# Pooled attention before two feed-forward stages: the tails of v pooled once per batch, and later groups' probabilities turned by one block transpose and a trip through DRAM

## The chip, the cores and the metric

The kernel runs on one core of one Trainium2 chip. The metric is device microseconds of one launch. Three runs of the kernel before took 1480.33, 1483.54 and 1484.5 us; the median is 1483.54 us.

## What is computed

```python
def _attn_ref(q, k, v):                     # 8 batches, 8 heads, 576 rows, 64 columns, float32
    k_p = k.reshape(B, H, Sp, 8, D).mean(axis=3)      # 72 pooled keys
    v_p = v.reshape(B, H, Sp, 8, D).mean(axis=3)
    scores = scale * np.matmul(q, k_p.transpose(0, 1, 3, 2))
    attn = np.exp(scores - scores.max(-1, keepdims=True))
    attn = attn / (attn.sum(-1, keepdims=True) + 1e-09)
    return np.matmul(attn, v_p)
...
    x = attn_out.transpose(0, 2, 1, 3).reshape(4608, 512)
    x = ((x @ w1) * (x @ w2)) @ w3 @ w_out            # 512 -> 1024 -> 512
    h = x @ w_in                                      # 512 -> 2048
    return (h * sigmoid(1.702 * h)) @ w_out2          # 2048 -> 512
```

Inputs q, k, v are float32; the weights arrive as 64-bit floats and are converted on the chip.

## The kernel before, in words

Every product of a feed-forward stage is taken as three matmuls: an operand is split into a rounded part and a remainder, and `mm3` (lines 112 to 116) multiplies high by high, high by low and low by high. `split` (103 to 105) makes the parts: ACT copies the high part, DVE or POOL subtracts it to get the low part.

**Attention** is cut into 32 groups: group n is batch n // 4 and the pair of heads n % 4. A group goes through these steps:
- `g_load`, `v_load`: SP issues four DMAs of k, four of q (lines 229 to 232), one of v (249, 128 of the 144 pooled rows of the two heads) and one of v's tail (250, the last 16 pooled rows, into `vtr`).
- `g0`: DVE turns k and q in 32x32 blocks (255, 256), sums k over its 8 rows (258); ACT puts the sums into the block-diagonal `kbd`.
- `g1`, `g2`: TensorE makes the scores of 576 queries against 2 x 72 keys (278), DVE takes the maximum and subtracts (283, 285), ACT takes exp (294).
- `g3`: DVE sums, inverts, normalises (300 to 303). The result `s_t` has queries on partitions and 160 key columns (144 and padding). It must be turned so that keys are on partitions, in `p0` (128 keys) and `p1` (the other 16, in 32 partitions). For groups 0 to 3 TensorE turns it (in `g4`); for groups 4 to 31 DVE does, with 20 transposes of 32 partitions each (310 to 316), which also carry each 32x32 block to other partitions.
- `g_va`: POOL sums v over its 8 rows in three halvings (324, 325, 327), once for 128 partitions (`va`) and once for the tail (`vat`), then scales (329 with a mask, 332 for the tail). `g_vb`: ACT and POOL split the sums into `vm` and, for the tail, `vt` (two ACT copies, lines 340 and 341, and one subtraction on POOL, 342).
- `g4`: ACT copies the high parts of `p0` and `p1` (368, 370, 371), POOL makes the low parts (369, 372).
- `g6`: TensorE multiplies by v (380 to 383), ACT and DVE write the split result into the slots `x` of the first feed-forward stage (390, 391).

**Around it.** From the start, weights are converted by `Conv`: SP loads a tile (line 151), ACT, DVE and POOL work on it (166, 168, 169, 172). The product of w3 and w_out is formed meanwhile (508 and `mm3`), and the first groups run among these steps. Then comes a loop over nine blocks of 512 rows and eight slices f: per f, 24 matmuls against w1 and w2 (624), the copy and product of the two (638, 641), a split, and 12 matmuls of the next stage, two slices late (`x2_step`). Twice per f, `tick` advances the attention by a quarter of a group, so that a group takes two values of f; block j needs the groups of batch j complete. The last group ends with block 6. Then the pool of the attention is closed and its memory is reused for converting w_in and w_out2, and from line 670 on the second feed-forward stage runs.

The order in which each engine takes its instructions is fixed when the program is built: the framework orders them by a simulated time line (`schedule_with_timeline_sim=True`), starting from the order of the code. So a later group's steps can stand ahead of an earlier group's on one engine, and each engine, SP's DMA queue too, keeps its order when the chip runs.

Single-buffered tiles that matter here: `vr`, `vtr`, `p0`, `p1`, `s_t` (for groups from 4 on), `kT`, `qT`, `ph`, `pt`; the raw k and q share four buffers.

Of the kernel before, what the change touches and what calls it, by code (L numbers as in the profile page):

```python
# [7 lines left out]
F32 = mybir.dt.float32  # L8
F32R = mybir.dt.float32r
# [3 lines left out]
ALU = mybir.AluOpType  # L13
# [4 lines left out]
P = 128  # L18
# [4 lines left out]
def pooled_attention_moe_moe2(  # L23
# [18 lines left out]
    nc = tc.nc  # L42
    B, H, S, D = q.shape
    NT, DM = out.shape
    POOL = 8
    SK = S // POOL
# [3 lines left out]
    HP = H // 2  # L50
# [18 lines left out]
    dr_p = ctx.enter_context(tc.tile_pool(name="dr", bufs=1, space=DRAM))  # L69
# [121 lines left out]
    with pa_ctx:  # L191
        pa = pa_ctx.enter_context(tc.tile_pool(name="pa", bufs=1))
        cv_p[0] = pa


        mask = pa.tile([P, 2, D], F32, name="mask")
        nc.gpsimd.memset(mask, 1.0 / POOL)
        nc.gpsimd.affine_select(
            out=mask[:, 0], in_=mask[:, 0], compare_op=ALU.is_gt, fill=0.0,
            base=SK, pattern=[[0, D]], channel_multiplier=-1)  # L200
        nc.gpsimd.affine_select(
            out=mask[:, 1], in_=mask[:, 1], compare_op=ALU.is_ge, fill=0.0,
            base=-SK, pattern=[[0, D]], channel_multiplier=1)
# [9 lines left out]
        vtr = pa.tile([32, POOL * D], F32, name="vtr")  # L213
# [11 lines left out]
        g_q, g_k, g_v, g_s = {}, {}, {}, {}  # L225
# [17 lines left out]
        def v_load(n):  # L243
            if n >= NG:
                return
            b, hp = divmod(n, HP)
            vr = v[b, 2 * hp:2 * hp + 2].rearrange("h (s u) d -> (h s) (u d)", u=POOL)
            g_v[n] = pa.tile([P, POOL * D], F32, name="vr", tag="vr")
            nc.sync.dma_start(g_v[n], vr[:P])
            nc.sync.dma_start(vtr[:KT], vr[P:])  # L250

        def g0(n):
            kr, qr = g_k.pop(n), g_q.pop(n)
            kT = pa.tile([P, S], F32, name="kT", tag="kT")
            nc.vector.transpose(out=kT, in_=kr.rearrange("p g d -> p (g d)"))
            nc.vector.transpose(out=qT[:, :S], in_=qr.rearrange("p g d -> p (g d)"))
# [39 lines left out]
        def g3(n):  # L296
            r, s_t = g_s.pop(n), s_of(n)
            pv = s_t[:, :, :KW].rearrange("p t (a s) -> p t a s", s=SK)
            rv = r.rearrange("p (t a) -> p t a", a=2)
            nc.vector.tensor_reduce(out=rv, in_=pv, op=ALU.add, axis=AX.X)  # L300
            nc.vector.tensor_scalar_add(r, r, 1e-9)
            nc.vector.reciprocal(out=r, in_=r)
            nc.vector.tensor_tensor(
                out=pv, in0=pv, in1=rv.unsqueeze(3).to_broadcast([P, TT, 2, SK]), op=ALU.mult)
            p0 = pa.tile([P, TT, P], F32, name="p0", tag="p0")
            p1 = pa.tile([32, TT, P], F32, name="p1", tag="p1")
            g_s[n] = (p0, p1)
            if n < NPE:
                return
            for r in range(5):  # L310
                for c in range(4):
                    nt = TT if 32 * (c + 1) <= S - (TT - 1) * P else TT - 1
                    dst = p0[32 * r:32 * r + 32] if r < 4 else p1[:32]
                    nc.vector.transpose(  # L314
                        out=dst[:, :nt, 32 * c:32 * c + 32],
                        in_=s_t[32 * c:32 * c + 32, :nt, 32 * r:32 * r + 32])

        def g_va(n):

            vr, tr = g_v.pop(n), vtr  # L320
            a = pa.tile([P, 4 * D], F32, name="va", tag="va")
            at = pa.tile([32, 4 * D], F32, name="vat", tag="vat")
            for d, s in ((a, vr), (at, tr)):
                nc.gpsimd.tensor_tensor(out=d, in0=s[:, :4 * D], in1=s[:, 4 * D:], op=ALU.add)
                nc.gpsimd.tensor_tensor(
                    out=d[:, :2 * D], in0=d[:, :2 * D], in1=d[:, 2 * D:], op=ALU.add)
                nc.gpsimd.tensor_tensor(out=d[:, :D], in0=d[:, :D], in1=d[:, D:2 * D], op=ALU.add)
            vf = pa.tile([P, 2, D], F32, name="vf", tag="vf")
            nc.gpsimd.tensor_tensor(
                out=vf, in0=a[:, :D].unsqueeze(1).to_broadcast([P, 2, D]), in1=mask, op=ALU.mult)  # L330
            vtf = pa.tile([32, D], F32, name="vtf", tag="vtf")
            nc.gpsimd.tensor_scalar_mul(vtf, at[:, :D], 1.0 / POOL)
            g_v[n] = (vf.rearrange("p a d -> p (a d)"), vtf)
            v_load(n + 1)

        def g_vb(n):
            vf, vtf = g_v.pop(n)
            nc.scalar.copy(vm[:, 0], vf)
            nc.gpsimd.tensor_tensor(out=vm[:, 1], in0=vf, in1=f32(vm[:, 0]), op=ALU.subtract)
            nc.scalar.copy(vt[:32, D:], vtf)  # L340
            nc.scalar.copy(vt[64:96, D:], vtf)
            nc.gpsimd.tensor_tensor(
                out=vt[32:64, D:], in0=vtf, in1=f32(vt[:32, D:]), op=ALU.subtract)

        def g4(n):
            p0, p1 = g_s.pop(n)
            if n < NPE:
                ps, s_t = banks_of(n), s_of(n)
# [4 lines left out]
                w = S - T  # L353
# [12 lines left out]
            s0 = p0.rearrange("p t c -> p (t c)")[:, :S]  # L366
            s1 = p1.rearrange("p t c -> p (t c)")[:, :S]
            nc.scalar.copy(ph[:, 0], s0)
            nc.gpsimd.tensor_tensor(out=ph[:, 1], in0=s0, in1=f32(ph[:, 0]), op=ALU.subtract)
            nc.scalar.copy(pt[:32], s1)  # L370
            nc.scalar.copy(pt[32:64], s1)
            nc.gpsimd.tensor_tensor(out=pt[64:96], in0=s1, in1=f32(pt[:32]), op=ALU.subtract)

        def g6(n):
            b, hp = divmod(n, HP)
# [296 lines left out]
    with tc.tile_pool(name="pb", bufs=1, reuse_waits="tile") as pb, \  # L672
# [196 lines left out]
        x = x_first  # L869
# [259 lines left out]
```

## Time and profile before

| | |
|---|---|
| median of three runs | 1483.54 us |
| profiled execution, its own time | 1480.04 us |
| span of its instructions | 1478.3 us |
| TensorE (PE) busy in the span | 1437.1 us (97%) |
| VectorE (DVE) busy | 991.5 us (67%) |
| ScalarE (ACT) busy | 696.6 us (47%) |
| GpSimd (POOL) busy | 491.9 us (33%) |
| granted TensorE clock, mean | 0.994 |
| attention's last matmul | about 629 us after the start |

A busy matmul time is modelled and pipelined: two matmuls overlap in it. What ends a stage is therefore read from TensorE's idle time, and not from its busy time alone. In a list of instructions the number in square brackets is the idle time of the engine just before, with what ended it. A line such as 105 belongs to a helper that many steps call.

### The profile page before, as it was taken

The page shows a single profiled execution, that of the slowest core. Times are in us where ns is not written, and L with a number is a line of the kernel's source. Part 1 is how long each engine was busy: PE and PEld are TensorE (multiplying, and loading weights), DVE is VectorE, ACT ScalarE, POOL GpSimd, SP SyncE. Part 2 cuts the span into 40 slices and gives each one's busy share as a digit, 9 for nine tenths or more (in the row PEclk, how much of TensorE's full clock was granted, in tenths as well). Part 3 has the DMA queues.
Part 4 walks back from the last instruction along what each step waited for, and adds up shares of the span by engine and source line. Part 5 has one row for each costly group of instructions (what it writes and reads, how often), then busy time and mean ns, then how long its engine had stood idle before and what let it go on. Part 6 is the DMA issues. An engine that isn't in the chain of part 4 may idle for free.

```text
span 1478.3 us, 19409 instructions
## 1 busy us (share of the span) xinstructions
PE 1437.1 (97%) x6536; PEld 1188.0 (80%) x6536; DVE 991.5 (67%) x1728; ACT 696.6 (47%) x1212; POOL 491.9 (33%) x589
## 2 busy tenths in 40 slices
PE   5978999999999999999999999999999999999998
PEld 3766888888888888888888887888788888888886
DVE  7889998878787877645636345783559354954554
ACT  6974444434343434366635334652455244634442
POOL 8787865555555555357743200000000000000000
PEclk9989999999999999999999999999999999999999
DMA  9992333323232321089869978877677766785665
GB/s 275 243 227 41 65 81 61 77 49 77 47 75 48 74 41 37 29 295 337 329 230 391 330 240 306 292 213 225 200 237 223 224 199 216 241 237 179 196 213 141
DMA packets 294434, 267.63 MB, mean 181 GB/s; under 512 B 201664, under 2 KB 226240, under 8 KB 294336
## 3 DMA queue, kind: packets, MB, share of 16 engines
q1 hardware_dynamic: 291648, 265.09, 60.0%
q10 hardware_dynamic: 2688, 1.31, 0.3%
q8 instruction: 52, 0.85, 0.2%
q14 instruction: 46, 0.38, 0.1%
HBM read 209.72 MB, written 56.62 MB: 180 GB/s over the span
## 4 chain that ended last, share of the span: by engine, by line
PE 82%; DVE 7%; DMA 5%; ACT 2%; POOL 2%; issue 1%; SPq 1%; DVEq 0%; ACTq 0%; POOLq 0%
PE bk L709 39%; PE wk L114 8%; PE wk L116 8%; PE wk L115 8%; PE acc L114 4%; PE acc L115 4%; PE acc L116 4%; PE wk L278 2%; DMA wud<-wt 2%; DVE s L105 1%; DVE cv L169 1%; PE bk L114 1%; PE bk L115 1%; PE bk L116 1%; POOL cv L172 1%
## 5 line engine op out<-in xcount | busy, mean ns | idle before, releaser
L709 PE MATMUL bk<-xM,st 128*128 128x512 f32 x1140 | 269.1, 390 | 1.8 <-DMA st<-wind 1.3
L709 PE MATMUL bk<-mv,st 128*128 128x512 f32 x1104 | 258.7, 389 | 0.5 <-DMA st<-wud 0.5
L709 PEld LDWEIGHTS bk<-xM,st 128*128 128x128 f32 x1140 | 213.6, 188 | 48.0 <-issue 1.9
L709 PEld LDWEIGHTS bk<-mv,st 128*128 128x128 f32 x1104 | 207.1, 188 | 44.2 <-ACT mv L104 0.9
L114 PE MATMUL wk<-s,s 128*128 128x512 f32 x576 | 227.3, 396 | 6.1 <-DVE a L641 4.1
L116 PE MATMUL wk<-s,s 128*128 128x512 f32 x576 | 225.2, 391 | 0.9 <-DVE s L105 0.9
L115 PE MATMUL wk<-s,s 128*128 128x512 f32 x576 | 225.3, 392 | 0.1
L314 DVE STREAM_TRANSPOSE p<-s_t 32x160 f32<-32x160 f32 (+1 forms) x560 | 178.3, 318 | 10.5
L115 PE MATMUL acc<-s,s 128*128 128x512 f32 x352 | 141.2, 401 | 1.0 <-POOL s L105 0.8
L116 PE MATMUL acc<-s,s 128*128 128x512 f32 x352 | 140.7, 400 | 1.6 <-DVE s L105 1.6
L114 PE MATMUL acc<-s,s 128*128 128x512 f32 x352 | 134.1, 406 | 8.1 <-DVE s L105 5.4
L114 PEld LDWEIGHTS wk<-s,s 128*128 128x128 f32 x576 | 108.5, 189 | 30.1 <-DVE a L641 5.4
L116 PEld LDWEIGHTS wk<-s,s 128*128 128x128 f32 x576 | 108.5, 188 | 23.8 <-DVE s L105 1.1
L115 PEld LDWEIGHTS wk<-s,s 128*128 128x128 f32 x576 | 108.5, 188 | 22.1 <-DVE s L391 0.5
L105 POOL TENSOR_TENSOR s<-a,s 128x512 fp32r<-128x512 f32 x56 | 73.3, 1309 | 155.2 <-ACT s L104 121.4
L105 DVE TENSOR_TENSOR mv<-g,mv 128x1024 fp32r<-128x1024 f32 x80 | 97.8, 1222 | 32.5 <-ACT mv L104 31.0
L104 ACT CAST mv<-g 128x1024 fp32r<-128x1024 f32 x80 | 84.5, 1056 | 71.3 <-PE bk L709 70.8
L172 POOL TENSOR_TENSOR cv<-cv,s 128x512 int32<-128x512 int32 x72 | 100.8, 1408 | 33.6 <-DVE cv L169 24.2
L114 PEld LDWEIGHTS acc<-s,s 128*128 128x128 f32 x352 | 67.9, 194 | 23.3 <-ACT s L104 4.7
L116 PEld LDWEIGHTS acc<-s,s 128*128 128x128 f32 x352 | 67.9, 193 | 15.8 <-DVE s L105 2.7
L115 PEld LDWEIGHTS acc<-s,s 128*128 128x128 f32 x352 | 68.0, 193 | 14.4 <-POOL s L105 2.0
L638 ACT COPY a<-wk 128x512 f32<-128x512 f32 x72 | 42.1, 585 | 68.3 <-PE wk L116 68.1
(188 smaller groups left out, 2344.6 us busy)
## 6 DMA issues: line engine op xcount, KB each, us to landing
st<-wud SPq DMA_DIRECT2D x92, 512.0 KB, 4.3
st<-wind SPq DMA_DIRECT2D x66, 512.0 KB, 4.6
st<-wind SPq DMA_DIRECT2D x84, 256.0 KB, 3.8
s<-in_moe_w_dram SPq DMA_DIRECT2D x32, 512.0 KB, 6.5
wind<-s SPq DMA_DIRECT2D x32, 512.0 KB, 5.5
s<-in_moe_w_out_dram SPq DMA_DIRECT2D x24, 512.0 KB, 6.9
s<-wud SPq DMA_DIRECT2D x20, 512.0 KB, 4.3
kr<-in_k_dram SPq DMA_DIRECT2D x128, 72.0 KB, 2.5
```

Source lines behind the costliest of these rows:

```text
L104: nc.scalar.copy(dst[:, 0], src)
L105: lo_eng.tensor_tensor(out=dst[:, 1], in0=src, in1=f32(dst[:, 0]), op=ALU.subtract)
L114: nc.tensor.matmul(o, a[:, 0, a_sl], b[:, 0, b_sl], start=first, stop=False)
L115: nc.tensor.matmul(o, a[:, 0, a_sl], b[:, 1, b_sl], start=False, stop=False)
L116: nc.tensor.matmul(o, a[:, 1, a_sl], b[:, 0, b_sl], start=False, stop=last)
L169: nc.vector.tensor_scalar(out=wu, in0=e.bitcast(U32), scalar1=3, scalar2=None, op0=ALU.logical_shift_left)
L172: nc.gpsimd.tensor_tensor(out=w.bitcast(I32), in0=w.bitcast(I32), in1=lo_w.bitcast(I32), op=ALU.add)
L278: nc.tensor.matmul(sc[half][:, i * KW:(i + 1) * KW], qT[:, sl(tt)], mov, start=True, stop=True)
L314: nc.vector.transpose(out=dst[:, :nt, 32 * c:32 * c + 32], in_=s_t[32 * c:32 * c + 32, :nt, 32 * r:32 * r + 32])
L638: nc.scalar.copy(a, pa_)
L709: nc.tensor.matmul(o, w[:, x, m], b[:, y], start=first and n == 0, stop=last and n == 2, skip_group_check=True)
```

## The change

Two edits. First, the tails of v: one tile `vtr` of 128 partitions holds the tails of all four head pairs of a batch, each in its own 32 partitions. It is loaded by four DMAs at the batch's first group, pooled and split there once, and the later groups of the batch take their 32 partitions from it by three ACT copies per group. The sums of v are now made in place in `vr` and `vtr`, without `va` and `vat`; the mask shrinks to one column per head and is broadcast.

Second, from group 8 on (`NPT` = 8) the 20 transposes of 32 partitions are replaced by one transpose of all 128 partitions, which turns each 32x32 block but leaves it in its partitions; four DMAs write the result to DRAM and two read it back into `p0` and `p1` with keys on partitions. To make this work, `turn_q` places q's blocks in another order with two transposes in place of one, so that columns come in halves (`by_half`). In these groups the low parts of the probabilities are made on DVE and not on POOL.

```diff
-            nc.sync.dma_start(vtr[:KT], vr[P:])
+            if hp == 0:
+                for h in range(HP):
+                    nc.sync.dma_start(
+                        vtr[32 * h:32 * h + KT],
+                        v[b, 2 * h + 1, S - KT * POOL:].rearrange("(s u) d -> s (u d)", u=POOL))
+        NPT = 2 * HP
+        PC = TT * 32
+        def turn_q(n, qr):
+            if n < NPT:
+                nc.vector.transpose(out=qT[:, :S], in_=qr.rearrange("p g d -> p (g d)"))
+                return
+            dst = qT.rearrange("p (t h e j) -> p e h t j", h=2, e=2, j=32)
+            src = qr.rearrange("p (h g) d -> p h g d", h=2)
+            for e, g0_, g1_ in ((0, 0, TT), (1, TT, SB // 2)):
+                nc.vector.transpose(out=dst[:, e, :, :g1_ - g0_], in_=src[:, :, g0_:g1_])
...
-            for r in range(5):
-                for c in range(4):
...
+            if n < NPT:
+                for r in range(5):
+                    for c in range(4):
...
+                return
+            turned = pa.tile([P, 5, TT, 32], F32, name="pT", tag="pT")
+            nc.vector.transpose(
+                out=turned.rearrange("p r t j -> p t r j"),
+                in_=s_t.rearrange("p t (r k) -> p t r k", k=32))
+            d = dr_p.tile([5, 32, 4, PC], F32, name="pD", tag="pD", bufs=2)
+            for c in range(4):
+                nc.sync.dma_start(
+                    d[:, :, c].rearrange("r k x -> k r x"),
+                    turned[32 * c:32 * c + 32].rearrange("p r t j -> p r (t j)"))
+            nc.sync.dma_start(
+                p0.rearrange("p t c -> p (t c)"), d[:4].rearrange("r k c x -> (r k) (c x)"))
+            nc.sync.dma_start(
+                p1.rearrange("p t c -> p (t c)"), d[4].rearrange("k c x -> k (c x)"))
...
-            vr, tr = g_v.pop(n), vtr
-            a = pa.tile([P, 4 * D], F32, name="va", tag="va")
-            at = pa.tile([32, 4 * D], F32, name="vat", tag="vat")
-            for d, s in ((a, vr), (at, tr)):
...
+            vr, first = g_v.pop(n), n % HP == 0
+            for d in (vr, vtr) if first else (vr,):
+                for w in (4 * D, 2 * D, D):
+                    nc.gpsimd.tensor_tensor(
+                        out=d[:, :w], in0=d[:, :w], in1=d[:, w:2 * w], op=ALU.add)
             vf = pa.tile([P, 2, D], F32, name="vf", tag="vf")
...
+            if first:
+                vtf = vtr[:, D:2 * D]
+                nc.gpsimd.tensor_scalar_mul(vtf, vtr[:, :D], 1.0 / POOL)
+                vtq[0] = pa.tile([P, 2, D], F32R, name="vtq", tag="vtq")
+                split(vtq[0], vtf, nc.gpsimd)
...
-            nc.scalar.copy(vt[:32, D:], vtf)
-            nc.scalar.copy(vt[64:96, D:], vtf)
-            nc.gpsimd.tensor_tensor(
-                out=vt[32:64, D:], in0=vtf, in1=f32(vt[:32, D:]), op=ALU.subtract)
+            for i, half in enumerate((0, 1, 0)):
+                nc.scalar.copy(vt[32 * i:32 * i + 32, D:], f32(tail[:, half]))
...
+            late = n >= NPT
+            lo = nc.vector if late else nc.gpsimd
...
+            lo.tensor_tensor(out=by_half(ph[:, 1]), in0=s0, in1=by_half(f32(ph[:, 0])), op=ALU.subtract)
...
+            lo.tensor_tensor(
+                out=by_half(pt[64:96]), in0=s1, in1=by_half(f32(pt[:32])), op=ALU.subtract)
```

## Rows read from the trace of the kernel before

**Rows 1.** Busy time by stage: stretch, its length, each engine's, granted clock, DMA.
```profile
0.00:212.00 212.00, 180.86 (x840) 144.25 (x841) 184.82 (x340) 135.16 (x284) 165.28 (x202) 0.96 0.68 160
212.00:610.00 398.00, 398.00 (x1921) 336.69 (x1920) 320.75 (x786) 157.86 (x352) 209.00 (x297) 1.00 0.26 56
610.00:1478.00 868.00, 858.27 (x3779) 707.09 (x3777) 485.97 (x604) 403.59 (x576) 117.64 (x91) 1.00 0.75 244
```

**Rows 2.** What PE waited for in 0 to 212 us: total, times, longest.
```profile
PE wk L508 <- POOL cv L172: 10.6, 2, 9.2
PE acc L114 <- DVE s L105: 5.4, 3, 2.9
PE wk L114 <- DVE a L641: 4.1, 2, 2.2
```

**Rows 3.** PE in order of time around 81 us: start, duration, idle before.
```profile
81.08 0.61 PE L114 MATMUL acc<-s,s 128*128 128x512 f32 x1 [2.90 <-DVE s L105]
81.49 0.63 PE L115 MATMUL acc<-s,s 128*128 128x512 f32 x1
81.92 0.63 PE L116 MATMUL acc<-s,s 128*128 128x512 f32 x1
```

**Rows 4.** The chain that ended last, the score matmuls of two successive groups.
```profile
399.25 1.23 PE wk L278 x10
417.93 1.23 PE wk L278 x10
```

**Rows 5.** DVE's groups of instructions, 250 to 600 us: busy us, mean ns, idle.
```profile
L314 DVE STREAM_TRANSPOSE p<-s_t 32x160 f32<-32x160 f32 (+1 forms) x378 | 120.4, 319 | 7.5
L255 DVE STREAM_TRANSPOSE kT<-kr 128x576 f32<-128x576 f32 x17 | 13.0, 765 | 0.0
L301 DVE TENSOR_SCALAR nm<-nm 128x10 f32<-128x10 f32 x19 | 3.3, 174 | 0.7
```

**Rows 6.** POOL's groups of instructions, 0 to 212 us.
```profile
L372 POOL TENSOR_TENSOR pt<-p,pt 32x576 fp32r<-32x576 f32 x9 | 13.5, 1504 | 0.9 <-POOL ph L369 0.3
L324 POOL TENSOR_TENSOR vat<-vtr 32x256 f32<-32x256 f32 x11 | 8.4, 764 | 0.2 <-DMA vtr<-in_v_dram 0.2
L325 POOL TENSOR_TENSOR vat<-vat 32x128 f32<-32x128 f32 x11 | 5.3, 484 | 0.0
L332 POOL TENSOR_SCALAR vtf<-vat 32x64 f32<-32x64 f32 x11 | 5.1, 460 | 0.0
L342 POOL TENSOR_TENSOR vt<-vtf,vt 32x64 fp32r<-32x64 f32 x10 | 5.0, 503 | 0.8
L327 POOL TENSOR_TENSOR vat<-vat 32x64 f32<-32x64 f32 x11 | 4.1, 375 | 0.0
```

**Rows 7.** DVE's group of line 301 in 0 to 212 us.
```profile
L301 DVE TENSOR_SCALAR nm<-nm 128x10 f32<-128x10 f32 x10 | 7.6, 764 | 0.2
```

**Rows 8.** One late group in order of time: normalising, last low part, product with v.
```profile
406.68 0.90 DVE L303 TENSOR_TENSOR s_t<-s_t,nm 128x720 f32<-128x720 f32 x1
...
416.53 1.42 POOL L372 TENSOR_TENSOR pt<-p,pt 32x576 fp32r<-32x576 f32 x1
...
425.16 0.29 PE L380 MATMUL wk<-ph,vm 128*128 128x288 f32 x1
```

**Rows 9.** ACT's copies of line 340 in 250 to 600 us.
```profile
L340 ACT CAST vt<-vtf 32x64 fp32r<-32x64 f32 x19 | 4.6, 241 | 0.0
```

**Rows 10.** Four DMA issues of one group's k on SP's queue: start, duration.
```profile
401.70 1.93 SPq L229 DMA_DIRECT2D kr<-in_k_dram  x4
```

**Rows 11.** Landing of the 256 KB stores of tile x2o to DRAM.
```profile
DMA to landing us min/median/max: 2.2/2.6/5.8
```

**Rows 12.** DMA issues of v: count, size, median us to landing.
```profile
vr<-in_v_dram SPq DMA_DIRECT2D x32, 256.0 KB, 2.8
```

**Rows 13.** SP's load of group 5's v, and POOL's last read of group 4's.
```profile
109.24 0.81 SPq L249 DMA_DIRECT2D vr<-in_v_dram  x1
...
114.76 0.45 POOL L329 TENSOR_TENSOR vf<-va,mask 128x128 f32<-128x128 f32 x1
```

More of the change, by code (lines that the diff above doesn't have):

```diff
@@ L193, in pooled_attention_moe_moe2 @@
         cv_p[0] = pa
-        mask = pa.tile([P, 2, D], F32, name="mask")
+        mask = pa.tile([P, 2], F32, name="mask")
         nc.gpsimd.memset(mask, 1.0 / POOL)
         nc.gpsimd.affine_select(
-            out=mask[:, 0], in_=mask[:, 0], compare_op=ALU.is_gt, fill=0.0,
-            base=SK, pattern=[[0, D]], channel_multiplier=-1)
+            out=mask[:, 0:1], in_=mask[:, 0:1], compare_op=ALU.is_gt, fill=0.0,
+            base=SK, pattern=[[0, 1]], channel_multiplier=-1)
         nc.gpsimd.affine_select(
-            out=mask[:, 1], in_=mask[:, 1], compare_op=ALU.is_ge, fill=0.0,
-            base=-SK, pattern=[[0, D]], channel_multiplier=1)
+            out=mask[:, 1:2], in_=mask[:, 1:2], compare_op=ALU.is_ge, fill=0.0,
+            base=-SK, pattern=[[0, 1]], channel_multiplier=1)
         qT = pa.tile([P, TT * P], F32, name="qT")
@@ L212, in pooled_attention_moe_moe2 @@
             nc.gpsimd.memset(t[:, :, KW:], 0.0)
-        vtr = pa.tile([32, POOL * D], F32, name="vtr")
+        vtr = pa.tile([P, POOL * D], F32, name="vtr")
         nc.gpsimd.memset(vtr, 0.0)
@@ L255, in g0 @@
             nc.vector.transpose(out=kT, in_=kr.rearrange("p g d -> p (g d)"))
-            nc.vector.transpose(out=qT[:, :S], in_=qr.rearrange("p g d -> p (g d)"))
+            turn_q(n, qr)
             ks = pa.tile([P, SK], F32, name="ks", tag="ks")
@@ L309, in g3 @@
                 return
[L310 to L327 removed]
+            if n < NPT:
+                for r in range(5):
+                    for c in range(4):
+                        nt = TT if 32 * (c + 1) <= S - (TT - 1) * P else TT - 1
+                        dst = p0[32 * r:32 * r + 32] if r < 4 else p1[:32]
+                        nc.vector.transpose(
+                            out=dst[:, :nt, 32 * c:32 * c + 32],
+                            in_=s_t[32 * c:32 * c + 32, :nt, 32 * r:32 * r + 32])
+                return
@@ new lines, in g3 @@
+            turned = pa.tile([P, 5, TT, 32], F32, name="pT", tag="pT")
+            nc.vector.transpose(
+                out=turned.rearrange("p r t j -> p t r j"),
[5 more added lines that the diff above has]
+                    turned[32 * c:32 * c + 32].rearrange("p r t j -> p r (t j)"))
@@ L328, in g_va @@
             vf = pa.tile([P, 2, D], F32, name="vf", tag="vf")
             nc.gpsimd.tensor_tensor(
[L330 to L333, printed above, removed]
+                out=vf, in0=vr[:, :D].unsqueeze(1).to_broadcast([P, 2, D]),
+                in1=mask.unsqueeze(2).to_broadcast([P, 2, D]), op=ALU.mult)
@@ L334, in g_va @@
+            if first:
[3 more added lines that the diff above has]
+                split(vtq[0], vtf, nc.gpsimd)
+            g_v[n] = (vf.rearrange("p a d -> p (a d)"), vtq[0][32 * (n % HP):32 * (n % HP) + 32])
             v_load(n + 1)
         def g_vb(n):
-            vf, vtf = g_v.pop(n)
+            vf, tail = g_v.pop(n)
             nc.scalar.copy(vm[:, 0], vf)
@@ L365, in g4, with by_half @@
             g_s[n] = (ph, pt)
[L366 to L372, printed above, removed]
+            late = n >= NPT
+            lo = nc.vector if late else nc.gpsimd
+            def by_half(ap):
+                return ap.rearrange("p (h x) -> p h x", h=2) if late else ap
+            s0, s1 = (by_half(t.rearrange("p t c -> p (t c)"))[..., :HALF if late else S]
+                      for t in (p0, p1))
+            nc.scalar.copy(by_half(ph[:, 0]), s0)
+            lo.tensor_tensor(out=by_half(ph[:, 1]), in0=s0, in1=by_half(f32(ph[:, 0])), op=ALU.subtract)
+            nc.scalar.copy(by_half(pt[:32]), s1)
+            nc.scalar.copy(by_half(pt[32:64]), s1)
+            lo.tensor_tensor(
+                out=by_half(pt[64:96]), in0=s1, in1=by_half(f32(pt[:32])), op=ALU.subtract)
         def g6(n):
```

2 lines of the change are left out of this document (1 added, 1 removed).

## The prediction, made before the changed kernel ran

> **What bounds the kernel now.** I read the busy time by stage first [rows 1]. From 212 to 610 us, where groups 8 to 31 (but for their first and last steps) run beside the first feed-forward stage, TensorE is busy 398.00 of 398.00 us at a granted clock of 1.00; DVE has 77 us free there, ACT 240, POOL 189. From 610 us on TensorE idles 9.7 of 868 us, and none of that is attention's. Only before 212 us is there something to win: TensorE idles 31.1 of 212 us, at a mean clock of 0.96. The list of its waits there [rows 2] splits this: 10.6 us until POOL's integer add at line 172 (9.2 of it the very first wait, for the first weights), then DVE's split at line 105 (5.4) and DVE's product at line 641 (4.1). Each stall also costs clock: after the 2.90 us wait that ends at 81.08 us the next 512-column matmuls start 0.43 us apart (81.49, 81.92) [rows 3], while a whole group's 72 such matmuls and its 18 smaller ones fit into 18.68 us, from 399.25 to 417.93 us [rows 4], under 0.26 us for each of the 72. That stage is full, and the early one waits for DVE.
>
> **Part 1, the tails of v: POOL.** Now every group does five tail instructions on POOL (lines 324, 325, 327, 332, 342): by their means in the early stage 764 + 484 + 375 + 460 + 503 = 2586 ns [rows 6]. Afterwards only a batch's first group does them, the last as the subtraction of the new split. Of the 11 groups whose sums fall before 212 us, numbers 0, 4 and 8 keep them: of 8.4 + 5.3 + 5.1 + 5.0 + 4.1 = 27.9 us [rows 6], 27.9 x 8/11 = 20.3 us go, an eighth of POOL's 165 us there [rows 1].
>
> POOL's own time releases TensorE seldom, but DVE is slower while POOL works: the same ten-column addition at line 301 lasts 764 ns before 212 us [rows 7] and 174 ns later [rows 5], so 0.59 us of it is waiting. The trace does not say how much of DVE's other work is such waiting, nor how much of it the tail instructions make. Bounds for the gain: nothing, if POOL's other work fills the freed time; and all of the 9.5 us that rows 2 show under lines 105 and 641, with as much again for the clock (0.04 of 212 us is 8.5 us), 18 us in all. An eighth less POOL work should take away about an eighth of each, 18 / 8 = 2.2 us; nearer to the lower end, because the weights' conversion stays the greater part of POOL's work. I take **2 us of gain**.
>
> The Trainium skill, page "GPSIMD Engine Reference", section Specifications, says that GpSimd's memory interfaces are shared with VectorE and that instructions with two SBUF inputs, or in a two-port mode, contend. Line 301 agrees (764 against 174 ns). Taken strictly the rule also counts the low parts that the change moves from POOL to DVE as still contending, so its sum is the same 2 us here, and it only speaks for the faster rival below.
>
> **Part 1, the rest.** ACT makes three small copies per group in place of two, and one more per batch: 40 of 0.24 us [rows 9], 10 us beside TensorE, which hides them in the full stage; early, a quarter of a microsecond per group on an engine that is busy 135 of 212 us [rows 1]. If that cover failed it would be 8 x 0.24 = 2 us and no more. The number of tail DMAs stays 32 (four per batch); their bytes too. The first batch's other three come ahead of the first group instead of one by one. At four issues in 1.93 us [rows 10] that is 1.5 us on SP's queue, given back at groups 1 to 3; I take zero.
>
> The sums in place keep `vr` until line 329 has read it, while now line 324 frees it. SP's next load of v waits that much longer, with the k and q of later groups queued behind it. In the full stage a group takes 18.68 us and SP's queue stands empty most of it: zero. Early it can cost; see the rivals.
>
> **Part 2, removed from groups 8 to 31.** 24 x 20 transposes of 319 ns [rows 5]: 153 us of DVE's time. The two low parts, at up to 1504 ns [rows 6], leave POOL: 24 x 3.0 = 72 us. All of it lies beside a TensorE that idles 0.00 us from 212 to 610 us [rows 1], so the gain is **zero**; what is late next there is again TensorE itself. Only group 8's part before 212 us counts at all, and I leave it in the 2 us.
>
> **Part 2, added.** One transpose of 800 columns. The trace has one of 576 columns in 765 ns [rows 5], so 765 x 800/576 = 1.06 us; bounds 0.9 us (the 720-column product at line 303 [rows 8]) and 20 x 0.319 = 6.4 us, should its four-dimensional pattern cost as much as the pieces. I take 1.06, since the q and k transposes are the same instruction. The second q transpose: the same columns in two pieces, bounded by another 0.77 us. Low parts on DVE: two, each at most the 0.90 us of line 303, which has more columns. DVE's net per group: 6.4 gone, 1.06 + 0.77 + 1.80 = 3.6 added.
>
> The trip, from the end of normalising at 406.68 + 0.90 = 407.6 us in the group shown [rows 8]: 1.1 for the transpose, 1.9 for four issues [rows 10], 2.6 until the last of four 102 KB stores has landed (the 256 KB stores: 2.2 to 5.8 [rows 11]), 0.4 for an issue, 2.8 for the read of 328 KB (v's 256 KB [rows 12]), together 8.8: `p0` stands at 416.4 us. Then ACT's three copies and the last low part on DVE, 4 x 0.9 = 3.6 at most: 420.0. Now the last low part ends at 416.53 + 1.42 = 418.0, and the product with v that reads it starts at 425.16 us [rows 8]. The new path is 2 us later and still 5.2 us early: **zero**. SP waits for DVE and then for its own stores; behind it stand the next v (needed by POOL most of a group later) and the stores of x2o, whose buffers are four. ACT waits for `p0` at line 368, with the copies of lines 638 and 104 behind; it waits there today for the transposes, without stopping TensorE. Traffic: 24 x 0.82 MB; per group 0.82 MB in 18.7 us is 44 GB/s on top of 56, at a DMA share of 0.26 [rows 1].
>
> **Sum.** 2 us off the profiled execution's 1480.04 us (span 1478.3): 1478.0. That execution lies 3.5 us under the median of the three runs, 1483.54 us, so the median afterwards is **1481.5 us**. A measurement of this kernel can tell about 0.3% from no change, 4.5 us.
>
> **The rivals.** *The early stalls dissolve.* If tail instructions stand just where DVE is waiting for POOL, most of the 9.5 us of rows 2, and the low clock that follows each stall, can go: half of the 18 us, 9 to 10 us, gives 1474 us. For it: DVE is busy 185 of 212 us, swollen by waits as at line 301. Against: DMA works at a share of 0.68 in this stage and the weights still have to arrive, and the freed eighth of POOL's time is spread over eight groups. By the skill's rule on the shared interfaces, just cited, this is the direction. Chance 0.28.
>
> *The trip is late.* Place: the product with v of each late group. Each microsecond beyond the 5.2 us of slack stops TensorE 24 times. It decides from a trip of 14 us (8.8 + 5.2). With the transpose at 6.4 and the store at 5.8 us the trip is 17.3 us, 3.3 too late, 79 us in all; at half a microsecond too late it is 12 us, 1493 us. For it: four DMA landings and SP's in-order queue lie in the path. Against: every row is a median or worse and the slack is over half of the trip. The Trainium skill, page "VectorE: DVE Perf Modes", section The three transpose paths, warns that a plain DMA which transposes by strides is 19 times slower than the hardware's own transposing DMA, when the innermost step at the destination is large. Here the innermost run is 160 adjacent numbers, since DVE turns the blocks beforehand; no row of before has this pattern. Chance 0.12.
>
> *SP stands behind v.* Early, SP would issue group 5's v not at 109.24 us but after 114.76 + 0.45 = 115.2 [rows 13], 6.0 us later, with q of the next group behind it; if DVE runs dry of q for that long, TensorE stalls 6 us and some clock, 8 us: 1491 us. The order of the queue is fixed at build time, and it may place that load later by itself. Chance 0.10.
>
> *It does not do what it says*: were the one transpose no faster than the twenty, only the trip would lengthen by 5.3 us, about its slack; the time would be the forecast's, and this lies inside it.
>
> **How the numbers follow.** Forecast (within 3 us of 1481.5): 0.50; early stalls dissolve: 0.28; late trip: 0.12; SP behind v: 0.10. The range reaches over the second and most of the fourth, 1471 to 1492, and leaves out most of the late trip and the far end of the first rival. Faster by over 0.3% is the first rival, 0.28; slower the other two, 0.22; within it 0.50.
>
> **What would show it.** Right: TensorE still idles 0.00 us in the stage of the late groups, DVE's busy time there falls by about 24 x 2.8 = 67 us, POOL's by some 72 and the tails; line 301 before 212 us falls under 764 ns; TensorE's early idle time is 29 us or a little less. Wrong: a wait of lines 380 to 383 for DVE or ACT in late groups (the trip), a wait of early matmuls that ends in a q transpose (SP's queue), or TensorE's idle time before 212 us down by 5 us and more (first rival). The forecast falls if the late stage speeds up at all, since it has no idle time to give.

## The result, and the profile after

The changed kernel takes 1494.12 us (median of six runs, 1490.21 to 1498.14) where the kernel before took 1482.67 us beside it (six runs, 1480.33 to 1484.84). The ratio is 1.0073, with a 95% interval of 1.0054 to 1.0092: by the ratio it is 10.8 us slower, between 8.0 and 13.6. The forecast was 1481.5 us, within 3 us of no change, and its range ended at 1492.

The profiled execution (1494.48 us, span 1492.8) by stage, the three stretches of [rows 1] (the span itself goes on to 1492.8 us); columns as there (length, busy us of PE, PEld, DVE, ACT and POOL with their counts, granted clock, DMA share, GB/s):

```profile
0.00:212.00 212.00, 175.31 (x792) 138.45 (x793) 172.01 (x314) 134.90 (x287) 145.54 (x161) 0.92 0.66 159
212.00:610.00 398.00, 398.00 (x1921) 337.31 (x1921) 232.05 (x434) 163.43 (x383) 117.63 (x171) 1.00 0.43 103
610.00:1478.00 868.00, 859.99 (x3787) 709.43 (x3786) 481.06 (x593) 407.05 (x583) 116.58 (x89) 1.00 0.75 244
```

The middle row is as forecast: TensorE still idles 0.00 us from 212 to 610 us, while DVE has lost 88.7 us of work there (320.75 to 232.05) and POOL 91.4. All of that freed time is worth nothing, because it lies beside a full TensorE. The first row is where the time went. TensorE idles 36.7 us there for 31.1 and its granted clock is 0.92 for 0.96, though DVE and POOL have 12.8 and 19.7 us less to do; 792 of its instructions stand in the first 212 us where 840 did. The last product of the attention starts at 639.6 us (before: 629.7), the first product of the second feed-forward stage, line 748 now, at 862.8 (853.4), and the span ends 14.5 us later: 9.4 us are lost before that product and 5.1 us behind it.

What TensorE waited for before 212 us in the changed kernel (total, times, longest); lines 547, 294 and 430 were 508, 278 and 391:

```profile
PE wk L547 <- POOL cv L172: 14.4, 4, 9.3
PE wk L294 <- DVE s L430: 6.9, 3, 3.1
PE wk L114 <- ACT a L677: 3.2, 1, 3.2
```

Beside [rows 2], the waits for the conversion of weights have grown from 10.6 us in two to 14.4 in four, and the score products wait 6.9 us behind DVE's line 430, a wait that the list of before does not have. None of the three is for an operation that the change added, removed or moved. That was the puzzle for the experiments.

DVE's groups in the stretch from 212 to 610 us of the changed kernel (count, busy us, mean ns, idle before):

```profile
L336 DVE STREAM_TRANSPOSE pT<-s_t 128x800 f32<-128x800 f32 x22 | 22.2, 1010 | 0.7
L266 DVE STREAM_TRANSPOSE qT<-qr 128x256 f32<-128x256 f32 (+1 forms) x42 | 19.4, 463 | 0.0
L410 DVE TENSOR_TENSOR pt<-p,pt 32x576 fp32r<-32x576 f32 x21 | 16.8, 802 | 1.0 <-ACT pt L408 0.3
L407 DVE TENSOR_TENSOR ph<-p,ph 128x576 fp32r<-128x576 f32 x21 | 16.1, 767 | 112.6 <-ACT ph L406 112.6
```

The single transpose takes 1010 ns (forecast 1.06 us), q's two pieces 926 ns for the 765 of one, the low parts 767 and 802 ns (forecast at most 900). One late group in order of time, in the changed kernel (start, duration, engine, line), answers to [rows 8]:

```profile
380.54 0.90 DVE L319 TENSOR_TENSOR s_t<-s_t,nm 128x720 f32<-128x720 f32 x1
381.47 1.01 DVE L336 STREAM_TRANSPOSE pT<-s_t 128x800 f32<-128x800 f32 x1
382.51 1.79 SPq L341 DMA_DIRECT2D pD<-pT  x4
385.86 0.34 SPq L344 DMA_DIRECT2D p<-pD  x1
389.11 0.67 ACT L406 CAST ph<-p 128x576 fp32r<-128x576 f32 x1 [3.15 <-DMA p<-pD]
391.20 0.75 DVE L410 TENSOR_TENSOR pt<-p,pt 32x576 fp32r<-32x576 f32 x1
398.17 0.29 PE L419 MATMUL wk<-ph,vm 128*128 128x288 f32 x1
```

From the end of normalising at 381.44 us `p0` needs 7.7 us (forecast 8.8), the last low part is ready at 391.95, 10.5 us after it, and the first product of the group with v starts 6.2 us later. The trip keeps its slack in the full stage.

### The profile page after: what moved, and what is told of

Same layout as the page of the kernel before. It is cut to its first block, busy times and chain, and to the rows that moved or that the text cites. A ratio compares the mean times of both kernels' runs of the same rounds, so it can differ in the third digit from the quotient of the medians.

```text
span 1492.8 us, 19012 instructions
## 1 busy us (share of the span) xinstructions
PE 1442.6 (97%) x6536; PEld 1192.5 (80%) x6536; DVE 888.7 (60%) x1344; ACT 705.4 (47%) x1252; POOL 379.8 (25%) x421
## 4 chain that ended last, share of the span: by engine, by line
PE 83%; DMA 6%; DVE 6%; ACT 2%; SPq 1%; issue 1%; POOL 0%; DVEq 0%; ACTq 0%; POOLq 0%
PE bk L748 39%; PE wk L116 8%; PE wk L114 8%; PE wk L115 8%; PE acc L116 4%; PE acc L114 4%; PE acc L115 4%; PE wk L294 2%; DMA s<-in_moe_w_dram 2%; DVE p L331 2%; DMA wud<-wt 1%; DMA st<-wind 1%; PE bk L116 1%; PE bk L114 1%; PE bk L115 1%
## 5 line engine op out<-in xcount | busy, mean ns | idle before, releaser
L172 POOL TENSOR_TENSOR cv<-cv,s 128x512 int32<-128x512 int32 x72 | 100.0, 1397 | 35.1 <-DVE cv L169 21.6
L407 DVE TENSOR_TENSOR ph<-p,ph 128x576 fp32r<-128x576 f32 x24 | 18.4, 766 | 123.5 <-ACT ph L406 123.5
```

What stands on the lines that cost most here:

```text
L172: nc.gpsimd.tensor_tensor(out=w.bitcast(I32), in0=w.bitcast(I32), in1=lo_w.bitcast(I32), op=ALU.add)
L407: lo.tensor_tensor(out=by_half(ph[:, 1]), in0=s0, in1=by_half(f32(ph[:, 0])), op=ALU.subtract)
```

## The experiments

Four theories are named in the expectations. **A**: the tails' loads, now once per batch, stand in other places of SP's queue and push k, q and weights back. **B**: the way through DRAM stops TensorE, or SP. **C**: sums in place hold the one `vr` until the mask product has read it, so v comes late. **D**, formed after the first eight runs: none of these by its work; the build, which places instructions on a simulated time line, chose another order for the first 200 us. Microseconds in the text are the ratio's distance from 1 times the median of before in the same comparison (1482 to 1484 us).

### Each part alone

**e1**: the changed kernel without part 2.
```diff
-        NPT = 2 * HP
+        NPT = NG
```


> The first edit alone (tails once per batch, sums in place, small mask); no group's probabilities go through DRAM. Theory A (the loss is made before 212 us by the tails' edit, which gives SP's queue another order, so that the last weights are issued later): 10 to 15 us slower than the kernel before, as the full change, with TensorE's idle time before 212 us near 37 us and the mean clock near 0.92. Theory B (the trip through DRAM costs the time): within 3 us of the kernel before.

**e2**: before with the sums in place, the small mask and part 2; tails per group.
```diff
+            turn_q(n, qr)
...
-            a = pa.tile([P, 4 * D], F32, name="va", tag="va")
...
+            a, at = vr, tr
...
```


> The second edit alone (probabilities through DRAM from group 8 on); v's tails are loaded and pooled per group as before, though with the sums in place and the small mask, without which the new tile finds no room. Theory A: within 4 us of the kernel before, TensorE idle 0.00 us in the stage from 212 to 610 us. Theory B: 10 us slower or more, with waits of TensorE in late groups. Theory C (sums in place make SP wait for v's last reader): 6 to 10 us slower, by a longer early stage.

**e3**: before with nothing but the sums in place.
```diff
-            a = pa.tile([P, 4 * D], F32, name="va", tag="va")
-            at = pa.tile([32, 4 * D], F32, name="vat", tag="vat")
+            a, at = vr, tr
...
```


> The kernel before with only v's sums made in place, tails still per group. Theory A: within 4 us of the kernel before, since SP's queue takes the weights in the same places as before. Theory C: 6 to 10 us slower, with SP waiting for POOL ahead of the loads of q.

**e4**: e1 with the sums out of place again.
```diff
-            for d in (vr, vtr) if first else (vr,):
+            for d, s in ((a, vr), (at, vtr)) if first else ((a, vr),):
...
```


> Tails once per batch and the small mask, but the sums out of place as before; no group goes through DRAM. Theory A: 8 to 15 us slower than the kernel before, since the four tail loads per batch are what moves SP's queue. Theory C: within 4 us of the kernel before.

Measured: e1 1489.91 us, 1.0047 (1.0030 to 1.0064); e2 1497.87, 1.0100 (1.0080 to 1.0119); e3 1496.93, 1.0093 (1.0077 to 1.0108); e4 1487.55, 1.0030 (1.0019 to 1.0040). No theory gave these four: by A e1 was to be 10 to 15 us slower and is 7.0 us, by C e3 was to be 6 to 10 us slower and is 13.8, and e2's 14.8 us come without the waits of late groups that B asked for. B falls: e2, which has the trip, is only 1 us over e3, which has not, and TensorE idles 0.00 us from 212 to 610 us in both. The smallest edit of all, e3, costs more than the whole change, 13.8 us against 10.8, and with the tails pooled once per batch the same edit costs far less (e1 is 2.5 us over e4). Costs that do not add up are a sign that something other than work is being changed. Part 2 shows most of its own loss behind 860 us: from the first product of the second feed-forward stage (the first that reads `xM`) to the end of TensorE's last e2 takes 4 us longer than before, e1, e3 and e4 at most 2.

What SP waited for in the first 140 us of e3, and two of TensorE's waits before 212 us:

```profile
SPq L229 <- DVE qT L256: 14.3, 2, 13.1
SPq L249 <- POOL vf L328: 8.9, 1, 8.9
```
```profile
PE acc L381 <- POOL vm L338: 5.1, 1, 5.1
PE acc L379 <- ACT vm L337: 3.2, 1, 3.2
```

It looked like theory C: SP stands 8.9 us until the mask product at line 328 has freed `vr`, v of groups 3 and 4 is issued at 99.74 and 122.90 us where it was at 88.43 and 99.97, and TensorE waits 8.3 us for the parts of v.

### Taking the hold away, and three variants of the whole change

**e5**: e3 with two buffers for v.
```diff
-            g_v[n] = pa.tile([P, POOL * D], F32, name="vr", tag="vr")
+            g_v[n] = pa.tile([P, POOL * D], F32, name="vr", tag="vr", bufs=2)
...
```


> Sums in place as in e3 (14.1 us slower than before), but two buffers for vr, so that the next group's v can be loaded while POOL still reads this one's. Theory C (the hold of the single vr is what costs): the 14 us go, 1483 us within 4; v of the fourth and fifth group is issued before 100 us and the products with v (lines 379 to 383) no longer wait in 80 to 130 us. Rival (the additions in place are themselves slower on POOL, or the reordering of SP's queue costs whatever the hold): it stays at 1493 to 1498 us.

**e6**: the changed kernel; odd groups of the first two batches load v into memory that is idle until group 8.
```diff
+            if n < NPT and n % 2:
+                g_v[n] = pa.tile([P, 5 * TT * 32], F32, name="vr", tag="pT")[:, :POOL * D]
...
```


> The changed kernel (1494.1 us) with a second buffer for v in the first two batches: odd groups' v is loaded into the memory of pT, which is not used until group 8. Theory C with A: the part of the early loss that the hold makes (e1 less e4, 2.4 us) goes, the tails' place in SP's queue (4.7 us) and the late feed-forward stage (4 us) stay: 1489 to 1492 us. Rival (the hold makes all of the early loss): 1487 us, with TensorE's idle time before 212 us back at 31 us. Rival (the hold does nothing here, since the tails have reordered the queue already): 1494 us.

**e7**: the changed kernel; the first eight groups do their tails one by one and their sums out of place, as before.
```diff
+            if n < NPT:
+                both = pa.tile([P, 5 * TT * 32], F32, name="va", tag="pT")
+                a, at = both[:, :4 * D], both[:32, 4 * D:8 * D]
...
```


> The changed kernel with the first eight groups as in before (tails group by group, sums out of place, into the memory of pT); tails once per batch, sums in place and the way through DRAM from the ninth group on. If the early stage holds all of the loss except the 4 to 5 us that kernels with pD lost after 860 us: 1487 us, landmarks as in before up to 853 us and 4 us late at the end. If the late loss only follows from the early one: 1483 us. If the full stage costs anything after all, the first product of the second feed-forward stage is later than 853 us though the early windows are those of before: over 1488 us.

**e8**: the changed kernel with `pD` inside DRAM tiles that exist already.
```diff
-            d = dr_p.tile([5, 32, 4, PC], F32, name="pD", tag="pD", bufs=2)
+            d = wu_d[A11 if n % 2 else A12].rearrange("p f a u -> (p f a u)")[:20 * 32 * PC].rearrange(
+                "(r k c x) -> r k c x", r=5, k=32, c=4)
```


> The changed kernel (1494.1 us) with pD laid into DRAM tiles that exist already and are written only from 790 us on (wud), so that no DRAM tensor is added. Theory (the added tensor shifts where the weights lie in DRAM, and reads of wud after 860 us land later: 4.6 to 4.9 us for 4.3): 1490 us, the reads at 4.3 us again, 619 us from the first bk<-xM product to the end. Rival (the late loss comes from something else, the order of SP's queue or chance): 1494 us, reads at 4.6 us and more, 624 us.

Measured: e5 1506.76 us, 1.0159 (1.0139 to 1.0179); e6 1491.83, 1.0057 (1.0041 to 1.0072); e7 1497.02, 1.0095 (1.0076 to 1.0114); e8 1491.68, 1.0058 (1.0037 to 1.0080). Both theories missed e5: with the hold gone it became slower still, by 23.6 us. The trace shows why. TensorE and DVE in e5, in order of time:

```profile
117.79 2.03 PE L278 MATMUL wk<-kbd,qT 128*128 128x144 f32 x10 [1.93 <-DVE qT L256]
136.05 0.88 PE L379 MATMUL wk<-ph,vm 128*128 128x288 f32 x2 [16.23 <-DVE s_t L285]
```
```profile
127.69 0.90 DVE L303 TENSOR_TENSOR s_t<-s_t,nm 128x720 f32<-128x720 f32 x1
128.62 6.65 DVE L314 STREAM_TRANSPOSE p<-s_t 32x160 f32<-32x160 f32 x20
135.30 0.97 DVE L285 TENSOR_TENSOR s_t<-wk,nm 128x432 f32<-128x432 f32 x2
```

TensorE stands 16.23 us in front of a product of one group with v, whose PSUM bank is freed by DVE's subtraction of the next group (line 285), and on DVE that subtraction stands behind all twenty transposes of a group. Every operation here has its usual length; it is their sequence that leaves TensorE idle. No run held e5's own order, so for e5 this rests on the trace alone. e7 says the same: the work of its first eight groups is that of before, and yet the attention in its profile ends 9.4 us late (last product at 639.05 us for 629.65), which none of the three cases written for it foresaw. e6 gives back 2.4 us, as the first of its cases had it; it says little, since the two intervals overlap and its order differs as well. e8 comes to its own below. So theory D was formed, and put to a test that changes the order and nothing else.

### The order alone

e3 and before consist of the same instructions, traced in the same sequence. Compared in the two built programs, their orders differ only early: on TensorE from its instruction 147 to 918, on DVE from 56 to 416, on SP from 44 to 382, and not at all behind that. So the order of one can be given to the other, by an edge from each instruction to the next on its engine that fixes their sequence and adds no wait for completion (`row` holds the places of an engine's instructions in the order wanted):
```diff
+        for x, y in zip(row, row[1:]):
+            tc.add_manual_dep(at[y], at[x].name, mybir.DependencyInfo(
+                mybir.DependencyClass.NoSync, mybir.DependencyReason.DATA), reason="order")
```
**e10** is e3 in the order of before, **e11** is before in the order of e3; the built orders are then identical, instruction by instruction, to those aimed at. **e12** is the changed kernel with all that it shares with before held in the order of before, **e13** the same with `pD` placed as in e8.

> The instructions of e3 (sums of v in place, single vr; 1496.9 us), but with the order in which they stand on each engine and on SP's queue fixed to that of before. Both programs trace the same instructions, so nothing but the operands of the sums and the wait of vr's load differs from before. Theory D (the cost is not the work, nor the hold of vr, but the order that the build chose for the first 200 us because of it): 1483 us within 4. Theory C (the hold of vr costs by itself): 1493 to 1497 us, with SP standing before the v loads and products with v waiting.

> The reverse: the kernel before with all its instructions and buffers (sums out of place), in the order that the build chose for e3. Theory D: slow as e3, 1493 to 1498 us, though no operation and no buffer differs from before. Theory C: 1483 us within 4, since vr is free after the first sum.

> The changed kernel (1494.1 us), all of its instructions, with those that it shares with before held in the order of before through the early stage (some 2400 of them; tail loads, the sums of tails and the new steps of the late groups go where the build puts them). Theory D: the early loss of 7 to 9 us goes, the 4 to 5 us after 860 us stay: 1486 to 1489 us, first product of the second feed-forward stage back at 853 to 855 us. Rival (the change's early work itself costs): 1491 us and more, that product at 860 us and later.

> e12 with pD laid into DRAM tiles that exist already (as in e8). If the added DRAM tensor makes the loss after 860 us by its place: 2 to 4 us under e12, 1483 to 1485 us, the reads of wud at 4.3 us. If that loss has another cause: the same as e12 within 2 us. If the tails' relief of POOL is worth anything at all in the early stage, this is the kernel that shows it: under 1481 us.

Measured: e10 1489.06 us, 1.0031 (1.0018 to 1.0044); e11 1497.10, 1.0089 (1.0076 to 1.0102); e12 1489.61, 1.0043 (1.0028 to 1.0059); e13 1487.00, 1.0023 (1.0011 to 1.0035). Before 212 us, first e3, then e11, then e10 (columns as in the first table):

```profile
0.00:212.00 212.00, 169.36 (x770) 135.07 (x771) 171.23 (x321) 130.18 (x272) 161.50 (x196) 0.90 0.63 151
```
```profile
0.00:212.00 212.00, 170.25 (x772) 135.88 (x773) 169.81 (x322) 130.30 (x272) 160.74 (x196) 0.90 0.63 151
```
```profile
0.00:212.00 212.00, 179.16 (x830) 142.20 (x831) 177.85 (x333) 134.59 (x283) 163.18 (x197) 0.96 0.65 156
```

e11 has every operation and buffer of the kernel before and is as slow as e3, 13.2 us against 13.8, with the same idle time and the same clock of 0.90. That the order by itself costs this much is shown. e10 has e3's work and the old order and keeps 4.6 us of the loss, a little over the 4 us that theory D allowed: the hold of `vr` is the likely rest (SP stands 21.5 us for line 328 in the first 140 us of e10, 17.5 of them once, and the first halving of `vr` takes POOL 733 ns there, 728 in before), but it is the smaller part. Before in its own order, held by the same edges, was not run; that the edges alone cost much is unlikely, since e15 below has them and is faster than before. For the change as it was made, e12 gives the order's part, since it has the changed kernel's work: 4.4 us (1.0073 less 1.0043; the two intervals just overlap), and TensorE's first 212 us are nearly those of before again, with 29.9 us idle at a clock of 0.95. It is a net figure: the held order brings 3.1 us of idle time between 212 and 610 us that the changed kernel does not have, and the first product of the second feed-forward stage starts at 858.6 us, between the 853 to 855 us that the expectation named for D and the 860 of its rival.

The placement of `pD` is seen twice in the time. The reads of the second stage's weights, `st<-wud`, also land later in every kernel with the added tile, in 4.5 or 4.6 us for 4.1 to 4.3 in all others. These are before, the changed kernel and e8 (count, size, median us to landing); e12 has 4.6, e13 4.3:

```profile
st<-wud SPq DMA_DIRECT2D x92, 512.0 KB, 4.3
```
```profile
st<-wud SPq DMA_DIRECT2D x92, 512.0 KB, 4.6
```
```profile
st<-wud SPq DMA_DIRECT2D x92, 512.0 KB, 4.3
```

From the changed kernel to e8, which have the same built order, it is 2.2 us (1.0073 less 1.0058), from e12 to e13 3.0 us (1.0043 less 1.0023). In each pair the intervals overlap, so this is supported by the two together, rather than settled by either.

The later landings do not show how the time is lost. These are TensorE's products that read those tiles, first in the changed kernel, then in e8 (count, busy us, mean ns, idle before):

```profile
L748 PE MATMUL bk<-mv,st 128*128 128x512 f32 x1104 | 258.9, 389 | 0.1
```
```profile
L749 PE MATMUL bk<-mv,st 128*128 128x512 f32 x1104 | 258.8, 389 | 2.2 <-DMA st<-wud 2.2
```

TensorE waits more for them where they land sooner. From the first product that reads `xM` to the end of TensorE's last it is 619.4 us in before, 624.5 in the changed kernel, 623.8 in e12, 622.7 in e8 (expected: 619) and 620.8 in e13; but it is 623.3 in e5 too, which has no added tile and lands these reads in 4.1 us. So a part of the late loss has another cause that no run looked for, and what it is about the place was not tried.

### What is left

e13 was still 3.4 us over before. TensorE idles 3.5 us in its stretch from 212 to 610 us; the stall that shows how stands in ACT's and TensorE's order of time in e13:

```profile
255.28 0.67 ACT L407 CAST ph<-p 128x576 fp32r<-128x576 f32 x1 [7.05 <-DMA p<-wud]
```
```profile
256.49 0.51 PE L114 MATMUL wk<-s,s 128*128 128x512 f32 x1 [1.44 <-ACT a L678]
```

ACT waits 7.05 us for `p` to come back from DRAM, the copy at line 678 (638 before) stands behind it, and TensorE behind that: the queue that the forecast named under "Part 2, added". In the changed kernel's own order this does not happen; in the old order, made for transposes on DVE, it does, at the first late groups. **e14** is e13 with the old order held only for what starts before 165 us. **e15** is e4 in the old order: the tails of part 1, without the sums in place and without the reordering.

> e13 (1487.0 us) with the order of before held only for what starts before about 165 us there; from the last early groups on the build orders the changed kernel by itself, so that the first late groups are spaced for their way through DRAM. Theory D with no cost of the change's own: the 3 to 3.5 us that e13 idles between 212 and 260 us go, 1483 to 1485 us, TensorE idle 0.0 us from 212 to 610 us. Rival (the change costs 3 us in the early stage by itself, whatever the order): 1487 us. Rival (a free order after 165 us loses elsewhere before 212 us): over 1488 us.

> e4 (tails once per batch, sums out of place, nothing through DRAM; 1487.6 us) with all that it shares with before held in the order of before. This is part 1 without its reordering: the forecast's 2 us of gain would give 1481 to 1483 us; the greater relief of the first rival, 1474 to 1478 us; no gain, 1484 us. If the first batch's three extra tail loads ahead of group 0 cost by themselves: 1486 us and more.

Measured: e14 1485.13 us, 1.0008 (0.9995 to 1.0022), no difference that this measurement can tell; e15 1480.56 us, 0.9980 (0.9968 to 0.9992), 3.0 us faster than before (1.2 to 4.7). e13 itself had missed the 1483 to 1485 us of its expectation, but lies within the 2 to 4 us under e12. The expectation for e14 held for the time and not for the trace: its profiled execution, the longest of its twelve (1489.87 us), still idles 3.45 us from 212 to 610 us. So how much of e13's remainder is that stall stays open. e15 is the only kernel of the study that is faster than before; its time lies 0.4 us under the 1481 to 1483 us that its expectation named for a gain of 2 us. Its first 212 us, and DVE's ten-column addition there, the line of [rows 7]:

```profile
0.00:212.00 212.00, 181.78 (x841) 144.52 (x842) 178.72 (x341) 139.29 (x297) 151.13 (x168) 0.97 0.67 162
```
```profile
L317 DVE TENSOR_SCALAR nm<-nm 128x10 f32<-128x10 f32 x10 | 4.8, 482 | 0.2
```

POOL works 14.2 us less than in [rows 1], DVE 6.1 us less for the same instructions, TensorE idles 30.2 us for 31.1, at a clock of 0.97 for 0.96. The 3 us stand on the times alone: the profiled execution of before is one of its fastest, and in the two profiles the attention ends at the same moment (last product at 629.65 and 629.66 us).

The last pair asks which order costs in e11. **e16** is before with SP's queue alone in e3's order, **e17** before with the four engines in e3's order and SP's queue in its own.

> The kernel before, its own instructions; SP's queue in the order that the build chose for e3, all five engines otherwise in the order of before. If the loss of e11 (13 us) comes from the queue (v of a group and some k and q stand later among the weights): 1493 to 1497 us. If it comes from the order in which the engines take their instructions: 1483 us within 3. If each makes half: about 1490 us.

> The other half: the kernel before with SP's queue in its own order, and TensorE, VectorE, ScalarE and GpSimd in the order chosen for e3. If the order on the engines makes the loss: 1493 to 1497 us. If the queue does: 1483 us within 3. If the two only cost together, because an engine's order was made for one queue: both halves over 1487 us.

Measured: e16 1505.50 us, 1.0146 (1.0123 to 1.0169); e17 1507.10 us, 1.0159 (1.0144 to 1.0174). Each half alone costs 21.6 and 23.6 us, more than both together (13.2). No case of e16's expectation foresaw such a time; the last case of e17's did, with over 1487 us for both. TensorE's two longest lists of waits before 212 us, first e16, then e17:

```profile
PE wk L508 <- POOL cv L172: 20.3, 4, 9.0
PE wk L114 <- ACT a L638: 6.1, 2, 4.6
```
```profile
PE wk L508 <- POOL cv L172: 10.9, 2, 9.6
PE wk L278 <- DVE s L391: 10.8, 2, 9.7
```

In e16 the engines take weights that the other queue brings late (20.3 us); in e17 they take scores in an order for which DVE's other work comes too late (10.8 us). Neither half of e3's order holds the loss by itself: engines and queue were laid out for each other, and what is lost is the fit.

## Why the prediction was wrong, by its own steps

**The bound.** Right. The stage of the late groups had no time to give, and gave none: TensorE's idle time there is 0.00 us before and after, with 88.7 us of DVE and 91.4 us of POOL gone. The forecast named 67 us of net relief for DVE, 2.8 per group. Per group 20 x 0.319 = 6.38 us went and 1.01 + 0.16 + 0.77 + 0.80 = 2.74 came, 3.6 net, 78 us for the 21 to 22 groups of the stretch; the other 10 us or so were not followed.

**Part 1, the tails.** The term "2 us of gain" came out in size: e15, where the tails change and the shared order does not, gains 3.0 us (1.2 to 4.7). By which way is not shown, since its profile and that of before reach the end of the attention together. The first rival, an early stage that dissolves to 1474 us, does not occur even with the order held. The sign that the step named, line 301's mean, does not serve. It falls from 764 to 482 ns in e15, but also to 521 ns in e11, which has all of POOL's work of before. Ten instructions make this mean, and in before they take from 157 to 2247 ns; the four longest each end 0.03 to 0.04 us after one of POOL's operations. Here is the first of them, with POOL's operation beside it:

```profile
30.75 2.25 DVE L301 TENSOR_SCALAR nm<-nm 128x10 f32<-128x10 f32 x1
31.68 1.28 POOL L172 TENSOR_TENSOR cv<-cv,s 128x512 int32<-128x512 int32 x1
```

The addition ends at 33.00 us, POOL's operation at 32.96. The Trainium skill, page "GPSIMD Engine Reference", section Specifications, says that GpSimd shares its SBUF interfaces with VectorE. The trace agrees for such single instructions, but how long POOL is busy in all does not set the mean. In the change as made the gain is buried: e4, the same work in the order that the build chose for it, loses 4.4 us.

**Part 1, the rest.** This is the step that failed. It priced each edit with every instruction left in its place: "The first batch's other three come ahead of the first group … I take zero", and "Early it can cost; see the rivals", which gave 8 us at a chance of 0.10. The order of the early stage is an output of the build. Another order for the very same work is worth 13.2 us there (e11), and the one chosen for the changed kernel costs it 4.4 us (e12). The step had the sentence in hand, "the order of the queue is fixed at build time, and it may place that load later by itself", and used it only to doubt the rival.

**SP stands behind v.** The place was right in kind. In the old order the sums in place, with their hold of `vr`, cost 4.6 us (e10), with SP standing 17.5 us at line 249, three times the 6.0 us that the rival priced. But in e3 TensorE stopped at products with v, not because DVE "runs dry of q", and a second buffer made e3 slower (e5). In the changed kernel itself SP's wait for that line before 130 us is a single one of 4.7 us.

**Part 2.** The removed work was priced rightly at zero, and the trip too, at 7.7 us for 8.8 with 6.2 us of slack. Its stores of 100 KB land in 1.9 us, against the 2.6 that was taken from [rows 11]. The Trainium skill, page "VectorE: DVE Perf Modes", section The three transpose paths, warns of a plain DMA that transposes by strides; no such slowness shows here, where the runs are 640 bytes. What the step left out is the DRAM tile itself. By e8 and e13 it costs 2 to 3 us (the intervals of each pair overlap), and what the changed kernel loses late, 5.1 us, lies in a stage that starts at 863 us, when the last of these groups is long done, and that the forecast read as untouched.

Together, from the changed kernel over e12 and e13 to before: 4.4 us for the order, 3.0 for the place of `pD`, and 3.4 (1.6 to 5.2) that remain in e13, of 10.8 us. In that remainder lie a gain of about 3 us from the tails (e15), the hold of `vr` (4.6 us in e10, where the tails are still per group) and up to 3.5 us of stalls at the first late groups; how these three share it was not separated.

## What to carry to other kernels

Where a build step orders the instructions by a simulated time line, an edit in a crowded stage has two prices, its work and the order that it provokes, and the second can be several times the first. Measure them apart: hold the old order with issue-order edges, and give the new order to the old work; here holding it turned the tails of part 1 from a loss of 4.4 us (e4) into a gain of 3.0 (e15). Where a stage is full, work taken from other engines is worth nothing, and then any disturbance elsewhere decides the sign.

## What the runs showed that had not been expected

- Two orders that each do well can do badly in halves: 13.2 us over before for engines and queue together, 21.6 for the queue alone, 23.6 for the engines alone.
- More buffers made a kernel slower: a second `vr` took e3 from 1.0093 to 1.0159, with an order of its own.
- More idle time of TensorE goes with a lower granted clock of the same 212 us, though not strictly: 0.96 with 31.1 us idle in before, 0.92 with 36.7 in the changed kernel, 0.90 with 42.6 in e3, 0.97 with 30.2 in e15, but 0.95 with 29.9 in e12.
- Where intermediate data lies in DRAM showed in reads of other tensors, over 200 us after its last use: 4.5 or 4.6 us to landing with the added tile, 4.1 to 4.3 without it. TensorE's waits for these reads did not grow with it.
